# A gated attention unit feeding a feed-forward layer, on one core: doubling the staged z on ScalarE, loading u of two chunks on SyncE's queue, and moving four block sums into the next chunk

## The chip, the cores and the metric

The kernel runs on one core of one Trainium2 chip. The metric is device time in microseconds for one execution. Before the change it took 1172.94 us (median of three runs, 1172.82 to 1172.99). The profiled execution that all rows below come from took 1172.72 us, of which 1170.4 us are the span from the first to the last instruction.

A core has four compute engines that run side by side and meet only at semaphores: TensorE (PE: matmuls, and PEld: its weight loads), VectorE (DVE), ScalarE (ACT) and GpSimd (POOL). SyncE (SP) issues DMA transfers; POOL and ACT can issue them too. Each engine works through its own list of instructions in order, so an instruction that waits holds up all that stand behind it on the same engine.

## The reference

Eight sequences of 3008 tokens go through an attention whose scores are squared after a ReLU, without a softmax; the result is gated by `u` and goes through a feed-forward layer with a sigmoid-approximated GELU:

```python
# u, v: (8, 3008, 256)   z: (8, 3008, 64)   w_in: (256, 2048)   w_out: (2048, 256), all float32
scores = (1.0 / S) * np.matmul(z, z.transpose(0, 2, 1))
attn = np.maximum(scores, 0.0) ** 2
x = u * np.matmul(attn, v)            # (8, 3008, 256), then taken as (24064, 256)
h = x @ w_in
g = h * (1.0 / (1.0 + np.exp(-1.702 * h)))
out = g @ w_out                       # (24064, 256)
```

## The kernel before

**Tiling.** A batch (one of the eight sequences, `b` = 0 to 7) is cut into six chunks of 512 tokens (`NCH` = 6; the last chunk has 448) and into 24 blocks of 128 keys. For each chunk the kernel computes scores z zT (line 247, tile `sc`), applies the ReLU on ACT (line 260, `rl`) and squares on DVE (lines 266 to 297, `a`). Scores are symmetric, so a block that is needed the other way round is turned by a DMA transpose on SP's queue (line 323, `tt`). Then come attn times v (line 651, `o`) and the gate with u (`xt`).

**Three forms of one product.** In the batches 1 to 6 the chunks 3 and 4 use a scheme with seven instead of eight block products (`attend_rows` for chunk 3, `attend_split` for chunk 4). It needs sums and differences of attention blocks (`sa`, lines 418 to 436) and of value blocks (`vt`), all on DVE. Chunk 4 is the place of this change: `split(b, i)` is true for chunk 4 of the batches 1 to 6. It has 42 steps of two 256-column matmuls each (line 483, tile `oz`). Its partial results are copied out of PSUM by ACT (line 495, `ya`) and added up and gated by DVE (lines 497 to 505).

**The feed-forward layer is woven in.** One up-group (`up_group(b, q)`) is four matmuls of x w_in (line 706, tile `hg`, one of two PSUM buffers), the activation on ACT (line 719, `hg` to `gf`, two buffers), and a scaled cast to float16 (`gf` to `gt`), on DVE (line 725) or for chosen `q` on ACT (line 723). Sixteen up-groups (`LAGY` = 16, those of the chunks 0 and 1) run inside chunk 4, one every 2.4 steps; the other up-groups run after chunk 5, between the products with w_out (`pair_product`, line 879, tile `st`). These products use a seven-product scheme too, so the `gt` tiles need block sums on DVE: S1 (line 841), S2 (line 843), S4 (line 845) and S3 (line 836). The sums stand in a list, `SUMS`, in the order S1, S2, S4, S3, and `some_sums(most)` takes one from it, or two when more than `most` wait. Before the change, `up_group` calls it for q from 8 with q % 4 < 2 in chunk 4, which puts three S1 and two S2 on DVE late in chunk 4.

So an up-group is a loop of three engines: PE needs a free `hg`, which ACT frees; ACT needs a free `gf`, which the cast frees; the cast stands in DVE's list among sums, gates and transposes.

**Other work on the queues in chunk 4.** At step 4, POOL first executes a tiny copy, `hold` (line 1120), which waits until the last attention transposes have landed. Then, in this order, POOL issues four transfers of u for chunk 4 (`load_u`, line 207), four of z for the next batch (lines 160 and 163, into two staging tiles `zst`), copies each staging tile once within itself so that z stands there twice (line 174, 128x768 float16), and later issues four transfers of u for chunk 5. The second z tile takes the buffer of an output tile and waits for DVE's transpose `yo` of it (line 981). After each copy on POOL, SP issues a DMA transpose of the staging tile into `ZT` (line 175), and then the stores of `yo` (line 991), four in the odd batches and twelve in the even ones. The tile `ZT` is read by the score matmuls of the next batch, which begin at step 2 of chunk 5; the second half of `ZT` is read from step 41 on. DVE transposes u of chunk 4 (line 214, `ut`) at step 25 and u of chunk 5 at step 8 of chunk 5.

The order on every engine is the order in which the Python code emits the instructions (a manual schedule); there is no planner that moves them. Tables such as `TURNS` and `LOADS` map (chunk, step) to the work that is emitted there.

Of the kernel before, what the change touches and what calls it, by code (L numbers as in the profile page):

```python
# [15 lines left out]
def kernel(  # L16
# [13 lines left out]
    AF = mybir.ActivationFunctionType  # L30
# [6 lines left out]
    NJ = (S + P - 1) // P  # L37
# [3 lines left out]
    NCH = (S + CH - 1) // CH  # L41
    CB = CH // P
    NU = NJ // 2
# [121 lines left out]
    def load_z(b):  # L165
        ZT[b] = pz.tile([P, NJ, P], F16, name="ZT", tag="ZT")
        if b == 1:
            stage_z(b, NU, tag="y")
        if b > 1:
            for n0 in range(0, NJ, NU):  # L170
                stage_z(b, n0, tag="y")
        for n0 in range(0, NJ, NU):
            zst = ZS[n0]
            pool.tensor_copy(zst[:, :, 1, :], zst[:, :, 0, :])
            sp.dma_start_transpose(ZT[b][:, n0:n0 + NU], zst.rearrange("p n c d -> p (n c d)"))

    VB = 4

# [19 lines left out]
        return CH if i < NCH - 1 else LAST  # L198

    def load_u(b, i):  # L200
        eng = pool if b else sp
        n = width(i)
        uq = pu.tile([P, CH // QW, QW, NCC], F32, name="uq", tag="uq")
        src = u[b, i * CH:i * CH + n].rearrange("(q t) c -> t q c", t=QW)
        for k in range(P // QW):
            cs = slice(k * NCC * QW, (k + 1) * NCC * QW)
            eng.dma_start(uq[k * QW:(k + 1) * QW, :n // QW].rearrange("t q c k -> t q (c k)"), src[:, :, cs])  # L207
        UQ[b, i] = uq
# [140 lines left out]
    def split(b, i):  # L349

        return i == NCH - 2 and 0 < b < B - 1
# [339 lines left out]
    def up_group(b, q):  # L691
        s, r = divmod(q, 2 * NFG)
        pair = paired(b, s)
        if pair:
            fg, e = (TILES if q >= 2 * NFG or b else TILES0)[r // 2], r % 2
            if fg >= NFG // 2:
                e = 1 - e
            k = 2 * s + e
        else:
            k, fg = divmod(q, NFG)  # L700
        i, n = blocks(b)[k]
        hg = ps2.tile([P, FFG, CH], F32, name="hg", tag="ps2")
        for e in range(FFG):
            ff = fg * FFG + e
            for c in range(NCC):
                pe.matmul(  # L706
                    hg[:, e, :n], W1[:, c, ff * P:(ff + 1) * P], XT[b, i][:, c, :n],
                    start=(c == 0), stop=(c == NCC - 1),
                )
        if pair:  # L710
            if r % 2 == 0:
                GT[b, s, fg, "pair"] = pa.tile([P, FFG, 2, CH], F16, name="gt", tag="tt", bufs=14)
            g = GT[b, s, fg, "pair"][:, :, k % 2, :n]
        else:
            if fg % 2 == 0:
                GT[b, k, fg // 2] = pa.tile([P, CB, CH], F16, name="gt", tag="tt", bufs=14)
            g = GT[b, k, fg // 2][:, (fg % 2) * FFG:(fg % 2 + 1) * FFG, :n]
        gf = pw.tile([P, FFG, CH], F32, name="gf", tag="gf")
        act.activation(gf[:, :, :n], hg[:, :, :n], AF.Gelu_apprx_sigmoid, scale=1.0 / FSC)  # L719
        if pair and q >= LAGY:  # L720
            some_sums(3 if q % 2 else 8)
        if (q >= LAGY and q % 8 in (1, 3, 5)) or (split(b, NCH - 2) and q in (9, 13)):
            act.activation(g, gf[:, :, :n], AF.Copy, scale=FSC)  # L723
        else:
            dve.tensor_scalar(g, gf[:, :, :n], FSC, None, ALU.mult)  # L725
        if not pair or LAGY > q >= (LAGY // 2 if split(b, NCH - 2) else 0) and q % 4 < (2 if split(b, NCH - 2) else 3):
            some_sums(8)
        if pair:
            some = (("S1", "S2", "S3"), ("S4",))[r % 2] if fg >= NFG // 2 else ()
            SUMS.extend([(s, "S1 S2 S4 S3".index(m), lambda m=m: pair_sum(b, s, fg - NFG // 2, m)) for m in some])  # L730
            SUMS.sort(key=lambda x: x[:2])
            if r == 2 * NFG - 2 and s == NCH // 2 - 1:
                some_sums(8)
        elif fg in (NFG - 3, NFG - 1):
            SUMS.extend([(s, 0, x) for x in left_sums(b, k, fg == NFG - 1)])
# [258 lines left out]
                )  # L994

    LAGY = 2 * NFG
    HEAD = 2

    def pieces(b, i):
# [31 lines left out]
    }  # L1031
    CASTW = {(3, 8): 0, (3, 40): 2, (4, 8): 1, (4, 14): 3}
    LOAD = {(3, NJ + 20): 4, (4, NJ + 5): 5}
    LOADS = {(4, 4): 4, (4, NJ + 5): 5}

    FIRST_ZT, FIRST_CAST = {12: 4, 20: 5}, {5: 4, 13: 5}
    SCHED0 = {
# [45 lines left out]
    for b in range(B):  # L1083
# [7 lines left out]
        for i in range(NCH):  # L1091
# [6 lines left out]
            for n, step in enumerate(  # L1098
                attend_split(b, i) if split(b, i) else attend_rows(b, i) if rowed(b, i)
                else attend(b, i, b == 0 and i == 0)  # L1100
            ):
                if b == 0 and i == 0 and n in (5, 24):
                    load_u(0, n // 24)
                if b == 0 and i == 0 and n == 2:
                    copies = first_zt(3)
                if b == 0 and i == 0 and n == 3:
                    copies()
                if b == 0 and i == 0 and n in FIRST_CAST:
                    first_cast(FIRST_CAST[n], True)
                if b == 0 and i == 0 and n in FIRST_ZT:  # L1110
                    first_zt(FIRST_ZT[n])()
                if (i, n) in turn:
                    turn_u(b, turn[i, n])
                if (i, n) in ((3, 4), (4, 7) if more else (4, 14)) and LAST2:
                    LAST2.pop(0)()
                if (i, n) == (0, 22) and COPY:
                    COPY.pop(0)()
                if split(b, i) and n == 4:
                    hold = pw.tile([P, 2], F16, name="hold", tag="hold")
                    pool.tensor_copy(hold, TT[b, i, NCH - 1][:, ::2, 0, 0])  # L1120
                if (i, n) in load:
                    load_u(b, load[i, n])
                if b == 0 and (i, n) in CASTW:
                    cast_w(CASTW[i, n])
                if b == 0 and (i, n) in LOADW:
                    load_w(LOADW[i, n])
                if b == 0 and (i, n) == (NCH - 2, 6):
                    stage_z(1, 0, tag="yo", bufs=1)
                if more and (i, n) == (NCH - 2, 4 if b else 16):
                    load_z(b + 1)  # L1130
                if b == 0 and i == NCH - 1 and n in (8, 30, 42):
                    wsums.pop(0)()
                take(host, sched[i].get(n, 0))
                if split(b, NCH - 2):
                    for op in extra.get((i, n), ()):
                        op()
                if split(b, i):
                    step()
                if i == full(b) and n >= HEAD and (n - HEAD) * LAGY // (2 * NJ - 10) >= head and head < LAGY:
                    up_group(b, head)  # L1140
                    head += 1
                if not split(b, i):
                    step()
# [64 lines left out]
```

## Time and profile before

| | |
|---|---|
| median of three runs | 1172.94 us |
| profiled execution: time, span | 1172.72 us, 1170.4 us |
| PE busy | 1161.1 us, 99% of the span |
| DVE busy | 983.6 us, 84% |
| ACT busy | 894.9 us, 76% |
| POOL busy | 224.4 us, 19% |
| granted TensorE clock | 1.000 |

The rows of the profile give, for a group of equal instructions, the line, the engine, the operation, output and inputs by tile name, the shapes and the count; after the first bar the busy time in us and the mean of one in ns; after the second bar the idle time of the engine just before them and what ended it. The timeline gives the start and the duration in us, and consecutive equal instructions are merged. Busy PE is not the same as PE at full pace: the ends of matmuls are modelled and overlap the next one (a 512-column matmul is shown with 379 ns, but four of them start within 0.86 us), so a short delay between two matmuls is only seen in the distance of their starts. The view by windows gives for each stretch its length and the busy time of each engine in it.

Chunk 4 of the batches 1 to 6 starts (first matmul of line 483) at 203.8, 348.9, 491.8, 637.0, 780.3 and 925.4 us.

### The profile page before, as it was taken

Reading aid. Unit: us, or ns where it says so; the run is one execution under the profiler, and the core shown is the slowest. Engines: PE = TensorE matmul, PEld = TensorE weight load, DVE = VectorE, ACT = ScalarE, POOL = GpSimd, SP = SyncE. Lnnn points to the kernel's source line nnn. Section 1 sums busy time; section 2 is a strip of 40 time slices with the busy share of each in tenths; the row PEclk is TensorE's granted clock in tenths of the full one; section 3 lists DMA queues with packets and bytes.
Section 4 is the critical chain, followed back from the end, with each engine's and each line's share of the span. In section 5 each row is a group of like instructions: output and inputs, shape, how many; then the busy total and the mean of one; then the engine's idle time right before and its main releaser. Section 6 shows DMA issues by size and latency. Waiting matters only on the chain.

```text
span 1170.4 us, 22657 instructions
## 1 busy us (share of the span) xinstructions
PE 1161.1 (99%) x8656; PEld 611.3 (52%) x8656; DVE 983.6 (84%) x1680; ACT 894.9 (76%) x1043; POOL 224.4 (19%) x307
## 2 busy tenths in 40 slices
PE   9999999999999999999999999999999999999998
PEld 3544456544465445654446545575444654544446
DVE  6779879988799887999879997899978999664776
ACT  7888867788667887688876887768878688672785
POOL 3033200432004320042101431024210251001000
PEclk9999999999999999999999999999999999999999
DMA  9996399754996559976498655987559875698023
GB/s 219 202 161 106 81 174 156 101 91 94 173 151 100 91 108 173 144 111 88 96 166 157 104 87 109 175 140 109 88 106 173 135 118 83 118 171 138 1 37 73
DMA packets 459036, 143.59 MB, mean 123 GB/s; under 512 B 424624, under 2 KB 453040, under 8 KB 458928
## 3 DMA queue, kind: packets, MB, share of 16 engines
q1 hardware_dynamic: 402464, 102.36, 53.4%
q0 software_dynamic: 55104, 38.49, 20.5%
q8 instruction: 67, 1.10, 0.4%
q10 hardware_dynamic: 1360, 1.31, 0.4%
q14 instruction: 41, 0.34, 0.1%
HBM read 60.29 MB, written 24.64 MB: 73 GB/s over the span
## 4 chain that ended last, share of the span: by engine, by line
PE 84%; DVE 11%; ACT 2%; issue 2%; DMA 1%; DVEq 0%; ACTq 0%
PE o L651 29%; PE st L879 23%; PE hg L706 23%; PE sc L247 5%; DVE gt L725 3%; PE oz L483 1%; DVE sa L436 1%; ACT rl L260 1%; PE st L927 1%; DVE sa L430 1%; DMA tt<-a 1%; DVE yo L981 1%; PE yp L853 1%; DVE sa L432 1%; DVE tt L418 1%
## 5 line engine op out<-in xcount | busy, mean ns | idle before, releaser
L719 ACT ACTIVATE gf<-hg 128x1024 f32<-128x1024 f32 (+1 forms) x384 | 380.5, 1001 | 97.2 <-PE hg L706 64.1
L260 ACT ACTIVATE rl<-sc 128x1024 f16<-128x1024 f32 (+1 forms) x344 | 310.8, 941 | 132.1 <-PE sc L247 113.1
L706 PE MATMUL hg<-xt,W 128*128 128x512 f16 (+1 forms) x1408 | 353.4, 374 | 2.1 <-ACT gf L719 1.6
L651 PE MATMUL o<-a,V 64*128 64x512 f16 (+3 forms) x2110 | 271.8, 368 | 0.2 <-DVE a L291 0.2
L651 PEld LDWEIGHTS <-V 64*128 64x128 f16 (+1 forms) x3246 | 174.5, 94 | 174.3 <-issue 5.5
L725 DVE TENSOR_SCALAR gt<-gf 128x1024 f16<-128x1024 f32 (+1 forms) x276 | 193.6, 705 | 59.4 <-ACT gf L719 57.8
L706 PEld LDWEIGHTS <-W 128*128 128x128 f16 x1536 | 149.5, 98 | 160.0 <-issue 6.7
L291 DVE TENSOR_TENSOR a<-rl 128x1024 f16<-128x1024 f16 (+1 forms) x230 | 152.2, 670 | 65.7 <-ACT rl L260 64.6
L207 POOL DMA_DIRECT2D uq<-in_u_dram x168 | 121.0, 730 | 348.1 <-DVE ut L214 157.4
L651 PE MATMUL o<-tt,V 64*128 64x512 f16 (+1 forms) x906 | 119.4, 376 | 0.0
L247 PE MATMUL sc<-ZT 64*128 64x512 f16 (+3 forms) x688 | 117.9, 356 | 0.7 <-ACT ZT L145 0.4
L879 PEld LDWEIGHTS <-WT 128*128 128x128 f16 x736 | 72.0, 98 | 79.6 <-issue 0.6
L723 ACT ACTIVATE gt<-gf 128x1024 f16<-128x1024 f32 (+1 forms) x108 | 110.7, 1025 | 3.6
L879 PE MATMUL st<-gt,W 128*128 128x512 f16 (+1 forms) x368 | 89.9, 370 | 0.0
L879 PE MATMUL st<-s,WT 128*128 128x512 f16 (+1 forms) x368 | 89.1, 370 | 0.0
L879 PE MATMUL st<-gt,WT 128*128 128x512 f16 (+1 forms) x368 | 88.7, 370 | 0.0
L879 PEld LDWEIGHTS <-W 128*128 128x128 f16 x552 | 53.8, 98 | 58.2
L1120 POOL COPY hold<-tt 128x2 f16<-128x2 f16 x6 | 1.6, 265 | 428.2 <-DMA tt<-a 283.3
L896 DVE SCALAR_TENSOR_TENSOR y<-st,y 128x512 f32<-128x512 f32 (+1 forms) x69 | 45.8, 664 | 19.6 <-PE st L879 18.7
L843 DVE TENSOR_TENSOR s<-s,gt 128x1024 f16<-128x1024 f16 (+1 forms) x92 | 60.5, 658 | 0.8
L841 DVE TENSOR_TENSOR s<-gt 128x1024 f16<-128x1024 f16 (+1 forms) x92 | 60.2, 660 | 0.9
L845 DVE TENSOR_TENSOR s<-gt,s 128x1024 f16<-128x1024 f16 (+1 forms) x92 | 59.4, 663 | 1.6 <-DVE s L843 0.5
(128 smaller groups left out, 1278.8 us busy)
## 6 DMA issues: line engine op xcount, KB each, us to landing
out_dram<-yo SPq DMA_DIRECT2D x156, 128.0 KB, 2.8
uq<-in_u_dram POOLq DMA_DIRECT2D x140, 128.0 KB, 3.4
V<-in_v_dram POOLq DMA_DIRECT2D x35, 256.0 KB, 6.0
tt<-a SPq DMA_TRANSPOSE x232, 3.4
uq<-in_u_dram POOLq DMA_DIRECT2D x28, 112.0 KB, 4.9
out_dram<-yo SPq DMA_DIRECT2D x28, 96.0 KB, 4.5
uq<-in_u_dram SPq DMA_DIRECT2D x20, 128.0 KB, 4.3
wst<-in_moe_w_in_dram POOLq DMA_DIRECT2D x4, 512.0 KB, 6.1
```

Source lines behind the costliest of these rows:

```text
L207: eng.dma_start(uq[k * QW:(k + 1) * QW, :n // QW].rearrange("t q c k -> t q (c k)"), src[:, :, cs])
L247: pe.matmul(sc[:, r, :q1 - q0], zt[h, 2 * kp + r, :], zt[h].rearrange("d n p -> d (n p)")[:, q0:q1], start=True, stop=True,)
L260: act.activation(rl[:, :, :n], sc[:, :, :n], AF.Relu, scale=csc)
L291: dve.tensor_tensor(a[:, :, :n], rl[:, :, :n], rl[:, :, :n], ALU.mult)
L651: ins = pe.matmul(acc[c][:, :n], channels(V16[b][h, j], c), weights(b, i, j)[h], start=(k, m) == first[c], stop=(k, m) == final[c],)
L706: pe.matmul(hg[:, e, :n], W1[:, c, ff * P:(ff + 1) * P], XT[b, i][:, c, :n], start=(c == 0), stop=(c == NCC - 1),)
L719: act.activation(gf[:, :, :n], hg[:, :, :n], AF.Gelu_apprx_sigmoid, scale=1.0 / FSC)
L723: act.activation(g, gf[:, :, :n], AF.Copy, scale=FSC)
L725: dve.tensor_scalar(g, gf[:, :, :n], FSC, None, ALU.mult)
L841: dve.tensor_tensor(s_, a21, a22, ALU.add)
L843: dve.tensor_tensor(s_, ST[b, s, "S1", m], a11, ALU.subtract)
L879: pe.matmul(bank, right[:, ff], lhs[:, f], start=new and ff == 0, stop=ff == NFF // 2 - 1, skip_group_check=True,)
```

## The change

It has three parts, all in the batches 1 to 6.

1. The two copies that double the staged z move from POOL to ACT (`twice_z`, emitted at the steps 19 and 28 of chunk 4, each directly followed by its DMA transpose on SP). Batch 0, which stages z for batch 1, keeps the copies on POOL.
2. The eight transfers of u for the chunks 4 and 5 move from POOL's queue to SP's queue. Those of chunk 4 are still emitted at step 4, those of chunk 5 at step 24 instead of 29.
3. No block sum is emitted by `up_group` in chunk 4 any more (`HEADSUMS` is empty). Four S1 sums are emitted in chunk 5, at the steps 18, 22, 26 and 30. The cast of up-group 9 moves from ACT to DVE; that of up-group 13 stays on ACT.

On TensorE the order of all instructions stays what it was. On DVE five sums leave chunk 4 (three S1, two S2), a cast is added there, four S1 are added in chunk 5, and the work after chunk 5 starts with four S2. On SP the order in chunk 4 becomes: u of chunk 4, stores of `yo`, first `ZT` transpose, u of chunk 5, second `ZT` transpose; before it was: first and second `ZT` transpose, stores of `yo`.

```diff
@@ load_z, new function twice_z
         if b > 1:
             for n0 in range(0, NJ, NU):
                 stage_z(b, n0, tag="y")
+            return
         for n0 in range(0, NJ, NU):
-            zst = ZS[n0]
+            twice_z(b, n0)
+
+    def twice_z(b, n0):
+        zst = ZS[n0]
+        if b > 1:
+            act.activation(zst[:, :, 1, :], zst[:, :, 0, :], AF.Copy, scale=1.0)
+        else:
             pool.tensor_copy(zst[:, :, 1, :], zst[:, :, 0, :])
-            sp.dma_start_transpose(ZT[b][:, n0:n0 + NU], zst.rearrange("p n c d -> p (n c d)"))
+        sp.dma_start_transpose(ZT[b][:, n0:n0 + NU], zst.rearrange("p n c d -> p (n c d)"))
@@ load_u
-        eng = pool if b else sp
+        eng = sp if b == 0 or (split(b, NCH - 2) and i >= NCH - 2) else pool
@@ up_group
-        if (q >= LAGY and q % 8 in (1, 3, 5)) or (split(b, NCH - 2) and q in (9, 13)):
+        if (q >= LAGY and q % 8 in (1, 3, 5)) or (split(b, NCH - 2) and q in (13,)):
             act.activation(g, gf[:, :, :n], AF.Copy, scale=FSC)
         else:
             dve.tensor_scalar(g, gf[:, :, :n], FSC, None, ALU.mult)
-        if not pair or LAGY > q >= (LAGY // 2 if split(b, NCH - 2) else 0) and q % 4 < (2 if split(b, NCH - 2) else 3):
+        if not pair or LAGY > q and (q in HEADSUMS if split(b, NCH - 2) else q % 4 < 3):
             some_sums(8)
@@ tables
+    HEADSUMS, LATESUMS = (), (18, 22, 26, 30)
...
-    LOADS = {(4, 4): 4, (4, NJ + 5): 5}
+    LOADS = {(4, 4): 4, (4, 24): 5}
+    TWICE = {19: 0, 28: 1}
@@ the loop over the steps of a chunk
+                if split(b, NCH - 2) and i == NCH - 1 and n in LATESUMS:
+                    some_sums(NCH * NFG)
+                if more and split(b, i) and n in TWICE:
+                    twice_z(b + 1, TWICE[n] * NU)
```

## The prediction

> **What bounds the kernel now.** I read the page first, then the windows of chunk 4, the waits in it, and the timeline of PE, DVE and POOL in batch 2.
>
> ```profile
> span 1170.4 us, 22657 instructions
> PE 1161.1 (99%) x8656; PEld 611.3 (52%) x8656; DVE 983.6 (84%) x1680; ACT 894.9 (76%) x1043; POOL 224.4 (19%) x307
> ```
>
> PE is the bound, and its order does not change. So the change can only move time where PE waits, and I look for those places. The windows run from the first to the last matmul of chunk 4 in the batches 1, 2 and 4:
>
> ```profile
> core 0: us, PE busy (x) PEld busy (x) DVE busy (x) ACT busy (x) POOL busy (x), PEclk, DMA share, GB/s
> 203.80:227.60 23.80, 23.51 (x149) 14.37 (x148) 23.03 (x39) 17.96 (x21) 12.48 (x15) 1.00 0.97 120
> 348.90:373.30 24.40, 23.55 (x151) 14.38 (x148) 23.63 (x40) 17.93 (x21) 11.69 (x15) 1.00 0.83 130
> 637.00:661.80 24.80, 23.78 (x149) 14.29 (x148) 24.03 (x39) 17.93 (x21) 12.21 (x15) 1.00 0.79 122
> ```
>
> The same work takes 23.8, 24.4 and 24.8 us, and DVE is busy for 97% of it (84% over the span). The waits of batch 2 in that window say what follows:
>
> ```profile
> ACT gf L719 <- DVE gt L725: 3.6, 5, 1.0
> PE hg L706 <- ACT gf L719: 0.8, 2, 0.6
> ```
>
> ACT waits for DVE's casts, PE for ACT. PE's loss is larger than these 0.8 us, because modelled ends hide short delays. The starts show it:
>
> ```profile
> 358.06 1.03 PE L706 MATMUL hg<-xt,W 128*128 128x512 f16 x4
> 358.93 0.60 PE L483 MATMUL oz<-sa,vt 128*128 128x256 f16 x4
> 359.70 1.02 PE L706 MATMUL hg<-xt,W 128*128 128x512 f16 x4 [0.17 <-ACT gf L719]
> ...
> 363.60 0.38 PE L483 MATMUL oz<-tt,vt 128*128 128x256 f16 x2
> 364.62 1.02 PE L706 MATMUL hg<-xt,W 128*128 128x512 f16 x4 [0.64 <-ACT gf L719]
> ```
>
> An up-group takes 0.86 us of PE (358.06 to 358.93), a 256-column matmul 0.108 (four between 358.93 and 359.36). So the up-group at 359.70 comes 0.34 us late and that at 364.62 0.81 us late.
>
> Chunk 4 at full pace is 83 x 0.108 + 16 x 0.864 = 22.8 us from its first to its last start. By the starts in the timeline the six batches take 23.77, 24.35, 23.77, 24.84, 23.76 and 24.03 us, 144.5 in all, against 136.7. **The loss that this change can reach is 7.8 us.** It stands in few places: in batch 1 (3 and 5 alike) 0.30 + 0.12 + 0.22 + 0.25, in batch 2 0.34 + 0.81 + 0.13 + 0.20, in batch 4 0.84 early and 1.14 later, in batch 6 0.24 and 0.91. All are ended by DVE, or by ACT behind DVE.
>
> What fills DVE, in batch 2, besides its own sums:
>
> ```profile
> 358.45 0.41 DVE L432 TENSOR_TENSOR sa<-sa,a 128x512 f16<-128x512 f16 x1
> 358.78 0.68 DVE L725 TENSOR_SCALAR gt<-gf 128x1024 f16<-128x1024 f32 x1
> 359.38 1.30 DVE L432 TENSOR_TENSOR sa<-sa,ad 128x512 f16<-128x512 f16 x1
> ```
>
> ```profile
> 359.56 0.83 POOL L174 COPY zst<-zst 128x768 f16<-128x768 f16 x1
> 361.58 1.00 POOL L174 COPY zst<-zst 128x768 f16<-128x768 f16 x1 [1.18 <-DMA zst<-in_z_dram]
> ```
>
> Two equal operations take 0.41 and 1.30 us; the second lies over POOL's copy. Under the second copy a 512-element L436 takes 1.04 us.
>
> **The change, part by part.**
>
> *The z copies leave POOL.* DVE gets back 0.89 + 0.63 us in batch 2, and 2 x 0.63 in batch 1, where two L436 take 1.04 us instead of 0.41. Weighed against the Trainium skill, "SBUF — State Buffer", section "Who interferes with whom": a DVE instruction with two SBUF inputs and a GpSimd instruction that reads SBUF exclude each other for the whole of whichever came first. By that rule the two copies would cost DVE up to their own 0.83 + 1.00 us, 0.3 us more than the rows; the sum would stay, since PE's loss caps it.
>
> *They land on ACT.* The nearest row is a cast of the same width, L723 at 128x768, 843 ns. Two copies are 1.69 us; the cast of up-group 9 (L723, 1.06 us) leaves. ACT goes from 17.9 to 18.6 us of a 22.8 us chunk. The tight place is step 19: between the up-groups 6 and 10 PE needs 5 x 0.86 + 10 x 0.216 = 6.5 us. ACT has five activations (0.91 to 1.02 us apart), two `ya` of 0.38 and the copy of 0.84 there: 6.2 to 6.7 us. Ends: nothing, or the whole 0.84 us per batch. I take 0.15, 0.9 us in six batches, because the two loads are level and ACT's waits for DVE (3.6 us in batch 2) shrink.
>
> The copy adds a wait on ACT: for z to land. Behind it stand the `ya` copy that frees a PSUM bank and all later activations. ACT reaches it about 11.2 us into the chunk. Before, the first z tile landed 10.3 to 11.4 us in (359.23, 214.82, 936.83). But its issue stood behind four u issues of 0.65 us on POOL, which are gone, so 2.6 us earlier. The second copy (step 28, about 16 us in) has z at 12.5 (361.43). Cost: nothing, hidden by those 2 to 3 us.
>
> *u goes to SP.* POOL loses eight issues of about 0.75 us in chunk 4. Casts beside such issues took 0.81 to 0.89 us instead of 0.68, so DVE gains some tenths more; I count none of it. On SP an issue of u takes 0.56 us (its rows of batch 0). SP had nothing to issue between 351.8 and 360.4 in batch 2. Its new order puts four u and up to twelve stores (6.87 us in one stretch of the timeline before) in front of the first `ZT` transpose. In batch 2: `yo` ends 356.33, stores until about 363.3, transpose issued by 364.8 instead of 361.9, landing 3.6 to 8.9 us after issue begins: 367 to 372.3. The first reader is the score matmul at 373.88, some 1.5 us earlier by then, 372.4. So it is hidden, with no margin at the far end. The second half is read only from step 41 on (about 383). u of chunk 5 is issued by 367 and read at 377.27.
>
> *The sums.* Three S1 and one S2 leave DVE in the window, 0.60 us from start to start each, the second S2 at its end; one cast of 0.60 us comes. In front of the last loss (`ya` at 369.90) DVE is ahead by 2 x 0.60 (sums) + 1.52 (copies) - 0.60 (cast) = 2.1 us in batch 2 and by 1.9 in batch 1. The losses behind the first copy are 1.14 and 0.89 us. So they go whole. What is late next is ACT at step 19, above.
>
> *What stays.* 0.34 in batch 2, 0.84 in batch 4 and 0.24 in batch 6 lie before the first copy and before any sum: DVE is behind there by `yo` and by casts of 1.05 and 1.22 us beside POOL's issues. z is still issued on POOL, u is not. Ends: all 1.4 us stay, or none. I take half, 0.7.
>
> *Chunk 5 and after.* Four S1 cost 4 x 0.60 = 2.4 us. In chunk 5 of batch 2 DVE idles 0.73 + 0.23 + 0.39 + 0.18 + 0.32 + 0.33 = 2.2 us behind ACT, and it enters the chunk without the S2 and its lag of about 1 us. So the gates at its end come no later: nothing. After chunk 5 one more sum is left to do than before; an idle gap of 0.85 us at 396.5 takes it. Without that cover it would cost 0.6 us per batch.
>
> Weighed against the move of u, the skill's "DMA: Bandwidth & Descriptors", section "Issuing engines are not separate DMA queues", holds that transfers from any engine end up on the same 16 DMA engines, so that another issuer saves only issue time. The rows: the DMA share in chunk 4 is 0.79 to 0.97 with u on POOL. By the rule the move speeds up no transfer and z would land no earlier than its issue allows; the sum, which counts no faster transfer, is the same.
>
> **Sum.** 7.8 - 0.7 - 0.9 = 6.2 us. The profiled execution took 1172.72 us (span 1170.4), so about 1166.5, with a span of 1164.2. The median of the runs is 0.2 above it: **1166.7 us**.
>
> **The rivals.**
> - *ACT becomes the bound of chunk 4.* For: ACT is level with PE at step 19 and has three `ya` in its list. Against: it idles 5.4 us in batch 2's window, mostly behind DVE. If each first copy costs its whole 0.84 us, 5.0 us come back: 7.8 - 0.7 - 5.0 = 2.1 to, at half that, 4.6 us gained; 1168.3 to 1170.8.
> - *The gain is given back behind chunk 4.* The sums fill DVE in chunk 5, or the first scores wait for `ZT` in the even batches (up to 1.6 us each if the landing takes 8.9 us). For: the margins are 0 to 1 us. Against: S1 is read only by the third product, and the median landing of `ZT` is 5.6 us. Three waits of 1.5 us, or 0.6 us in each of six batches, cost 3.6 to 4.5: 1170.3 to 1171.2.
> - *Slower: ACT stops at the z copy.* One mechanism: z lands late, and ACT, now in order behind it, starves PE of `hg`. The slack is 0.2 us (`ya` ended at 360.86, its bank is written again from 361.86, less the copy's 0.84); each us past it costs nearly 1 us per batch. It decides when z lands 1.7 + 0.2 us after ACT gets there, 13.1 us into the chunk: 10.1 us lost, 7.8 gained, 1175.2 and up. For it: `hold` and `yo` still stand before z. Against: the landings above, 10.3 to 11.4 with a later issue.
> - *It does not do what it says.* DVE's lag comes from its own list and not from what leaves: 0 to 2 us gained, 1171 to 1173. Against: the 0.41 and 1.30 us of two equal rows.
>
> **How the numbers follow.** A difference of 0.2% (2.3 us, faster below 1170.6) is about what a measurement of this kernel can tell from none. Chances: the forecast (1165.1 to 1168.3) 0.68; ACT as the bound 0.14; given back 0.09, two thirds of it still faster; z late 0.04; no effect 0.05. Faster 0.68 + 0.14 + 0.06 = 0.88, same 0.03 + 0.04 = 0.07, slower 0.04 + 0.01 = 0.05. The range: below, the whole 7.8 us and 0.3 for the runs, 1164.8; above, into the ACT case, 1170.0, which leaves out 0.15.
>
> **What would show it.** Right: chunk 4 takes 22.8 to 23.2 us in every batch, DVE about 83% busy in it; no L432 or L436 of 512 elements above 0.5 us; ACT's waits for the cast under 1.5 us; the distance from the last start of chunk 4 to the next batch's chunk 4 unchanged. Wrong: a new idle time of ACT in front of the z copies ended by a DMA; PE waiting for `ya` at step 22; a wait of the first scores for `ZT`; or chunk 5 longer by what chunk 4 lost.

## The result, and the profile after

The changed kernel takes **1166.65 us** (median of 13 runs, 1165.94 to 1171.88); the kernel before took 1173.01 us (median of 13 runs) on the same chip. The medians are 6.4 us apart; the ratio is 0.9952 with a 95% interval of 0.9941 to 0.9963. Ten of the thirteen runs lie between 1165.9 and 1167.1 us and three, of which there is no profile, at 1170.3 to 1171.9; of all executions below one, with u on POOL, took 1344.24 us at a granted clock of 0.85 and is left out. The forecast was 1166.7 us.

The profiled execution took 1165.94 us, its span is 1164.2 us. The first lines of the page, and its chain of work that ended last:

```profile
span 1164.2 us, 22650 instructions
PE 1157.7 (99%) x8656; PEld 611.6 (53%) x8656; DVE 978.5 (84%) x1686; ACT 898.0 (77%) x1049; POOL 178.7 (15%) x247
...
PE 97%; DVE 1%; ACT 1%; issue 0%; SPq 0%; DMA 0%; DVEq 0%; ACTq 0%
```

In the page of before that chain was PE for 84% and DVE for 11%. So nearly nothing that PE waits for is left: DVE's share is gone from the chain although DVE is as busy as before over the span (84%).

Chunk 4 is where the time went. The windows of chunk 4 in the batches 1, 2 and 4, with the columns as before:

```profile
core 0: us, PE busy (x) PEld busy (x) DVE busy (x) ACT busy (x) POOL busy (x), PEclk, DMA share, GB/s
204.00:226.90 22.90, 22.90 (x149) 14.39 (x148) 20.83 (x39) 18.75 (x23) 4.29 (x5) 1.00 0.95 125
348.20:371.20 23.00, 23.00 (x149) 14.40 (x148) 21.05 (x40) 18.65 (x23) 3.82 (x5) 1.00 0.92 130
633.90:657.00 23.10, 23.06 (x148) 14.38 (x148) 21.15 (x40) 18.57 (x23) 4.01 (x5) 1.00 0.94 134
```

From the first to the last start of a split product, the six chunks take 22.88, 22.92, 22.88, 23.11, 22.89 and 23.16 us, 137.8 in all instead of 144.5. That is 6.7 us; the span is 6.2 us shorter (of the other 0.5 us, 0.2 lie ahead of the first chunk 4 and 0.3 behind the last matmul). From the end of one chunk 4 to the start of the next it is 121.35 or 118.53 us, as before to 0.01 us: nothing is given back behind the chunk.

The starts of PE at the place in batch 2 where the up-groups had come 0.34 and 0.81 us late:

```profile
357.36 1.03 PE L713 MATMUL hg<-xt,W 128*128 128x512 f16 x4
358.22 0.60 PE L490 MATMUL oz<-sa,vt 128*128 128x256 f16 x4
358.66 1.02 PE L713 MATMUL hg<-xt,W 128*128 128x512 f16 x4
...
362.59 0.38 PE L490 MATMUL oz<-tt,vt 128*128 128x256 f16 x2
362.81 1.03 PE L713 MATMUL hg<-xt,W 128*128 128x512 f16 x4
```

Every distance is that of full pace: 0.86 for an up-group, 0.44 for four 256-column matmuls, 0.22 for two. DVE and ACT beside it:

```profile
358.34 0.41 DVE L439 TENSOR_TENSOR sa<-sa,ad 128x512 f16<-128x512 f16 x1
358.68 0.68 DVE L732 TENSOR_SCALAR gt<-gf 128x1024 f16<-128x1024 f32 x1
359.28 1.01 DVE L443 TENSOR_TENSOR sa<-tt,sa 128x1024 f16<-128x1024 f16 x2
359.43 0.83 ACT L179 ACTIVATE zst<-zst 128x768 f16<-128x768 f16 x1
360.17 0.38 ACT L502 ACTIVATE ya<-oz 128x256 f32<-128x256 f32 x1
360.43 1.03 ACT L726 ACTIVATE gf<-hg 128x1024 f32<-128x1024 f32 x1
```

L439 (L432 before) with `ad` takes 0.41 us where it took 1.30, and the casts take 0.68. The copy on ACT takes 0.83 us. The `ya` behind it starts at 360.17, 0.05 us after PE has finished its bank: ACT is in time, but only just. In the waits of that window, what ACT loses to DVE's casts:

```profile
ACT gf L726 <- DVE gt L732: 1.2, 2, 0.7
```

It was 3.6 us. What is left of PE's loss are 0.20 us in batch 4 and 0.25 us in batch 6, both 10.6 us into the chunk, behind a cast that lies beside POOL's issue of z (1.01 us in batch 4). A second profile of the same kernel (138.5 us for the six chunks) shows such early losses in the batches 1, 4 and 5 instead, 0.3 to 0.4 us each: where they fall, and how many, differs from one execution to the next.

### The profile page after: what moved, and what is told of

It is laid out like the page before. It is cut to its first block, busy times and chain, and to the rows that moved or that the text cites. A ratio compares the mean times of both kernels' runs of the same rounds, so it can differ in the third digit from the quotient of the medians.

```text
span 1164.2 us, 22650 instructions
## 1 busy us (share of the span) xinstructions
PE 1157.7 (99%) x8656; PEld 611.6 (53%) x8656; DVE 978.5 (84%) x1686; ACT 898.0 (77%) x1049; POOL 178.7 (15%) x247
## 3 DMA queue, kind: packets, MB, share of 16 engines
q10 hardware_dynamic: 1360, 1.31, 0.4%
## 4 chain that ended last, share of the span: by engine, by line
PE 97%; DVE 1%; ACT 1%; issue 0%; SPq 0%; DMA 0%; DVEq 0%; ACTq 0%
PE o L658 30%; PE hg L713 27%; PE st L886 23%; PE sc L254 6%; PE oz L490 4%; PE oz L548 4%; PE st L934 1%; PE yp L860 1%; ACT rl L267 0%; PE w L101 0%; DMA uq<-in_u_dram 0%; SPq L308 0%; DVE gt L732 0%; DVE yo L988 0%; ACT ZT L145 0%
## 5 line engine op out<-in xcount | busy, mean ns | idle before, releaser
L732 DVE TENSOR_SCALAR gt<-gf 128x1024 f16<-128x1024 f32 x282 | 194.8, 691 | 64.8 <-ACT gf L726 62.7
L214 POOL DMA_DIRECT2D uq<-in_u_dram x120 | 84.8, 720 | 382.6 <-DVE ut L221 170.8
L730 ACT ACTIVATE gt<-gf 128x1024 f16<-128x1024 f32 (+1 forms) x102 | 104.4, 1024 | 3.6
```

## The experiments

One number serves for all of them beside the medians: the sum of the six chunks 4 in the profiled execution. It is steadier than a single time, because everything between the chunks takes the same time to 0.01 us in all these profiles, while the stretches ahead of the first and behind the last chunk 4 differ in some, by waits for attention transposes, and a granted clock of 0.50 behind them, that no run here ties to the change (behind the last in the run without the moved sums 5.4 us longer, ahead of the first in the run with u on POOL 9.9 us). It is not exact either: two profiles of the changed kernel give 137.8 and 138.5 us, through their early losses. So a difference of 2 us counts here only where its loss stands at the same place in every batch; the intervals of the ratios of such runs overlap that of the changed kernel (0.9941 to 0.9963). Medians from different groups of runs, as their kernels before show (1173.0 to 1173.6), compare to about 0.6 us.

| kernel | median, us (runs) | before beside it | ratio, 95% interval | six chunks 4, us |
|---|---|---|---|---|
| before | 1173.01 (13) | | | 144.5 |
| z copies alone | 1169.92 (5) | 1173.62 | 0.9963 (0.9949 to 0.9977) | 141.2 |
| sums alone | 1172.03 (10) | 1173.62 | 0.9989 (0.9977 to 1.0001) | 142.3 |
| u alone | 1172.31 (10) | 1173.62 | 0.9989 (0.9980 to 0.9998) | 145.0 |
| the whole change | 1166.53 (4) | 1173.62 | 0.9933 (0.9918 to 0.9948) | 138.5 (137.8 above) |
| whole, z copies on POOL | 1173.33 (10) | 1173.34 | 0.9999 (0.9987 to 1.0011) | 143.4 |
| whole, sums in chunk 4 | 1168.97 (10) | 1173.34 | 0.9968 (0.9954 to 0.9982) | 140.0 |
| whole, u on POOL | 1168.47 (9) | 1173.34 | 0.9964 (0.9938 to 0.9989) | 140.0 |
| before, each POOL copy twice | 1181.44 (4) | 1173.34 | 1.0070 (1.0046 to 1.0093) | 153.2 |
| whole, each ACT copy twice | 1174.98 (10) | 1173.27 | 1.0015 (0.9990 to 1.0040) | 145.7 |
| whole, z issued late | 1191.93 (4) | 1173.27 | 1.0152 (1.0109 to 1.0194) | 163.2 |
| whole, cast 9 on ACT | 1169.86 (10) | 1173.27 | 0.9970 (0.9949 to 0.9991) | 140.1 |
| z copies and cast 9 | 1170.27 (10) | 1173.27 | 0.9969 (0.9951 to 0.9988) | 141.8 |

### The z copies alone

Against the kernel before, the copies move to ACT; u, sums and the cast of up-group 9 stay:

```diff
-            pool.tensor_copy(zst[:, :, 1, :], zst[:, :, 0, :])
+            twice_z(b, n0)
...
+        if b > 1:
+            act.activation(zst[:, :, 1, :], zst[:, :, 0, :], AF.Copy, scale=1.0)
...
+                if more and split(b, i) and n in TWICE:
+                    twice_z(b + 1, TWICE[n] * NU)
```

> The kernel before, with the doubling copies of z on ScalarE as the only part (u stays on POOL, the sums and the casts of the up-groups 9 and 13 stay where they were). Theory (VectorE's lag in chunk 4 costs PE its time, and each part takes some of that lag away): VectorE gets back 1.3 to 1.5 us per batch in front of the last loss, where 0.9 us are lost in the odd batches and 1.1 behind the first copy in the batches 2 and 4. So the losses behind the first copy go (5.9 us), and ScalarE, which keeps the second cast, may take 0.1 to 0.3 us per batch of it: 4.1 to 5.9 us gained, 1167.1 to 1168.9 against 1173.0. Rival (the sums were the load that mattered): 0 to 1.5 us gained. Rival (ScalarE becomes the bound): 0 to 3 us gained, with PE waiting for the copy of the partial result at step 22.

Measured: 3.7 us between the medians, 3.3 us in chunk 4, less than the 4.1 to 5.9 expected. All batches lose 0.35 us some 19 us into the chunk, at the second copy, 2.1 us together; the other 1.8 us are mostly early losses and, in the odd batches, 0.1 to 0.4 us behind the first copy. In the timeline of batch 1:

```profile
220.18 1.06 ACT L730 ACTIVATE gt<-gf 128x1024 f16<-128x1024 f32 x1
221.14 1.00 ACT L726 ACTIVATE gf<-hg 128x1024 f32<-128x1024 f32 x1
222.04 0.83 ACT L179 ACTIVATE zst<-zst 128x768 f16<-128x768 f16 x1
222.78 1.93 ACT L726 ACTIVATE gf<-hg 128x1024 f32<-128x1024 f32 x2
223.84 1.02 PE L713 MATMUL hg<-xt,W 128*128 128x512 f16 x4 [0.18 <-ACT gf L726]
```

ACT works without a gap from the cast of up-group 9 through the copy, and PE waits for it. So the largest part of the change alone does about half of the work, but ACT has no room for copy and cast together.

### The sums alone

Against the kernel before, only the sums move; the cast stays on ACT:

```diff
-        if not pair or LAGY > q >= (LAGY // 2 if split(b, NCH - 2) else 0) and q % 4 < (2 if split(b, NCH - 2) else 3):
+        if not pair or LAGY > q and (q in HEADSUMS if split(b, NCH - 2) else q % 4 < 3):
...
+                if split(b, NCH - 2) and i == NCH - 1 and n in LATESUMS:
+                    some_sums(NCH * NFG)
```

> The kernel before, with the block sums moved from chunk 4 to chunk 5 as the only part (z copies and u stay on POOL, both casts stay on ScalarE). Theory (VectorE's lag): two S1 stand in front of the last loss and one in front of the loss at about 17 us into the chunk, 0.60 us each; so nearly all of the 0.9 us goes in the odd batches and in batch 6, but the 0.81 us loss of the batches 2 and 4 lies before the first sum and stays: 3.5 to 4.3 us gained, 1168.7 to 1169.5. Rival (POOL's copies alone were the cause): 0 to 1 us gained.

Measured: 1.6 us between the medians, with an interval that reaches to no difference; chunk 4 is 2.2 us shorter. The batches 5 and 6 have no loss at all (22.90 us), 1 and 3 lose 0.65 us and 2 and 4 lose as much as before or more (1.8 and 2.0 us), most of it behind the POOL copies. The 3.5 to 4.3 us expected did not come. One thing that differs is where the POOL copies start: 11.3 to 13.7 us into the chunk in 5 and 6, 10.5 to 12.9 in the others. Over every copy one operation of DVE takes 1.04 us or more, in 5 and 6 too.

### u alone

```diff
-        eng = pool if b else sp
+        eng = sp if b == 0 or (split(b, NCH - 2) and i >= NCH - 2) else pool
...
-    LOADS = {(4, 4): 4, (4, NJ + 5): 5}
+    LOADS = {(4, 4): 4, (4, 24): 5}
```

> The kernel before, with u of the chunks 4 and 5 on SyncE's queue as the only part. Theory (VectorE's lag): only the casts beside POOL's issues get shorter, by 0.1 to 0.5 us each; the early losses of the batches 2, 4 and 6 (1.4 us together) shrink and the others stay: 0.3 to 1.5 us gained, 1171.5 to 1172.7. Rival (the order on the queues was what mattered: u and z earlier, the stores before the transposes): 4 us or more gained.

Measured: 1.3 us between the medians (interval 0.2 to 2.3), but chunk 4 of the profiled execution is not shorter (145.0). z lands earlier, so POOL's copies come earlier, and the losses behind them move forward (in the odd batches to 12.3 and 15.4 us into the chunk) instead of going. Where the 1.3 us would lie this profile does not show.

### The whole change beside its parts

The changed kernel again, beside the three on the same chip.

> The changed kernel as it is, for the same chip and the same rounds as its single parts. Every theory expects what it took before: 1166.6, between 1166 and 1167.5. Some of its executions took 1170 to 1172; if that belongs to the chip and not to the execution, all runs here agree among themselves within 0.3%. By the theory of VectorE's lag the parts add up to more than the whole (5 + 4 + 1 against 6.3 us), because each of them is enough for the same losses.

Measured: 7.1 us between the medians. The parts alone make 3.7 + 1.6 + 1.3 = 6.6, so they seem to add up (in chunk 4 less so: 3.3 + 2.2 - 0.5 = 5.0 of 6.0). The next three runs, which take one part away each, show that they don't.

### The whole change with the z copies on POOL

```diff
-        if b > 1:
-            act.activation(zst[:, :, 1, :], zst[:, :, 0, :], AF.Copy, scale=1.0)
-        else:
-            pool.tensor_copy(zst[:, :, 1, :], zst[:, :, 0, :])
+        pool.tensor_copy(zst[:, :, 1, :], zst[:, :, 0, :])
```

with `twice_z` called from `load_z` for all batches, as before the change.

> The whole change without its first part: u on SP and the sums moved as in the changed kernel, but both copies of z on POOL again, directly behind the z transfers. Theory A (the parts add up: alone they brought 3.7, 1.6 and 1.3 us against the runs of the kernel before beside them, 6.6 together, and the whole 7.1): without the copies on ScalarE 3.5 to 4 us are lost, 1169.8 to 1170.6. Chunk 4 then has losses of about 0.6 us per batch, near 1.2 us behind the start of the first copy, behind a VectorE operation that lies over a POOL copy and takes 1.0 us or more instead of 0.41. Theory B (a common lag: VectorE has to be behind by more than a reserve before PE loses anything, and the sums with the u issues free enough reserve): at most 1.5 us lost, 1167 to 1168; the operations over the POOL copies still take 1.0 us or more, but PE's starts show no loss behind them.

Measured: the time of the kernel before (ratio 0.9999). 6.7 us are lost between the medians, more than either theory had; in the profiled execution chunk 4 is 5.6 us longer. In every batch 0.65 to 1.2 us are lost behind the copies. Batch 2, with VectorE's operations over the two copies:

```profile
359.32 1.01 POOL L177 COPY zst<-zst 128x768 f16<-128x768 f16 x1
...
359.57 1.31 DVE L728 TENSOR_SCALAR gt<-gf 128x1024 f16<-128x1024 f32 x1
...
361.74 1.64 DVE L439 TENSOR_TENSOR sa<-tt,sa 128x1024 f16<-128x1024 f16 x2
361.84 1.25 POOL L177 COPY zst<-zst 128x768 f16<-128x768 f16 x1 [1.52 <-DMA zst<-in_z_dram]
361.89 0.38 ACT L498 ACTIVATE ya<-oz 128x256 f32<-128x256 f32 x1
362.05 1.02 PE L709 MATMUL hg<-xt,W 128*128 128x512 f16 x4 [0.40 <-ACT gf L722]
```

The cast takes 1.31 us instead of 0.68, the pair of L439 1.64 instead of 1.01. DVE has five sums less in this chunk and loses all the same. The copies come early here (the first 9.7 to 10.1 us into the chunk, against 10.6 to 11.9 before), and the first sum stood 16.8 us in (batch 2 before). That fits a reserve that stands behind the copies and cannot be spent ahead of time. It also leaves something open: with the sums moved, later copies on POOL cost nothing in two batches (the run with the sums alone), and no run here has the copies on POOL at the steps 19 and 28. So these runs do not part what the other engine brings from what the later place brings.

### The whole change with the sums in chunk 4

```diff
-        if not pair or LAGY > q and (q in HEADSUMS if split(b, NCH - 2) else q % 4 < 3):
+        if not pair or LAGY > q >= (LAGY // 2 if split(b, NCH - 2) else 0) and q % 4 < (2 if split(b, NCH - 2) else 3):
...
-    HEADSUMS, LATESUMS = (), (18, 22, 26, 30)
+    HEADSUMS, LATESUMS = (), ()
```

> The whole change without its third part, except the cast of up-group 9, which stays on VectorE: three S1 and two S2 are in chunk 4 again, none in chunk 5. Theory A (parts add up): 1.2 to 2.0 us lost, 1167.7 to 1168.5, and the loss in chunk 4 stands late, behind up-group 12 (18 us and more into the chunk), where the sums of up-group 8 and on have made VectorE late. Theory B (common reserve, the copies and u free enough of it): 0 to 0.5 us lost, 1166.3 to 1167.

Measured: 2.4 us lost between the medians, 2.2 us in chunk 4. Of these 1.9 us stand at one place, 20.3 to 20.6 us into the chunk, 0.30 to 0.35 us in each of the six batches; neither profile of the changed kernel has them. The waits of PE over the span, and the place in batch 1:

```profile
PE oz L490 <- DVE ya L508: 0.8, 4, 0.2
```

```profile
224.14 0.43 DVE L508 TENSOR_TENSOR ya<-ya,oz 128x256 f32<-128x256 f32 x1
224.21 0.27 PE L490 MATMUL oz<-tt,VZ 128*128 128x256 f16 x1
224.62 0.38 PE L490 MATMUL oz<-tt,vt 128*128 128x256 f16 x2
```

PE needs the bank that the addition of `ya` frees, and DVE comes to it late, after two casts in a row. The matmul starts 0.41 us after the one before it instead of 0.11. Theory A is right in place and, by these 1.9 us, in size (1.2 to 2.0 expected).

### The whole change with u on POOL

```diff
-        eng = sp if b == 0 or (split(b, NCH - 2) and i >= NCH - 2) else pool
+        eng = pool if b else sp
...
-    LOADS = {(4, 4): 4, (4, 24): 5}
+    LOADS = {(4, 4): 4, (4, NJ + 5): 5}
```

> The whole change without its second part: u of the chunks 4 and 5 is issued by POOL again. Theory A: what returns are the early losses that lie before the first copy (0.34 us in batch 2, 0.84 in batch 4, 0.24 in batch 6 before; 0, 0.2 and 0.25 after), 0.8 to 1.4 us: 1167.3 to 1168. In addition z is issued later by four u issues, so ScalarE reaches the first copy before z is there: if that matters, a wait of the first copy for the z transfer shows on ScalarE and each us of it costs up to 1 us in each of six batches, 1169 and up. Theory B (u counts for nothing, as my sum had it): 1166.4 to 1167.

Measured: 1.9 us lost between the medians, 2.2 us in chunk 4; so u seems to count, but this rests on less than the other parts, since the intervals overlap and the early losses vary. In the batches 2, 4 and 6 the early losses are back (0.57, 0.67 and 0.59 us, 1.8 together). In the six profiles here with u on POOL the losses up to 11.1 us into the chunk make 0.9 to 1.8 us, in the eight with u on SP 0 to 1.1 us. Batch 2 of this run shows one, behind a cast beside POOL's issue:

```profile
363.18 1.05 POOL L160 DMA_DIRECT2D zst<-in_z_dram  x1
363.54 1.20 DVE L732 TENSOR_SCALAR gt<-gf 128x1024 f16<-128x1024 f32 x1
...
365.41 0.60 PE L490 MATMUL oz<-sa,vt 128*128 128x256 f16 x4
...
366.19 1.02 PE L713 MATMUL hg<-xt,W 128*128 128x512 f16 x4 [0.18 <-ACT gf L726]
```

In the odd batches 0.1 to 0.4 us are lost some 13 us in. What ACT waited for ahead of its z copies (us in total, times, longest):

```profile
ACT zst L179 <- DMA zst<-in_z_dram: 0.6, 2, 0.4
```

So z issued later by four u issues comes up to 0.4 us too late for ACT in two odd batches. In the changed kernel ACT has no such wait.

### Each copy on POOL twice

```diff
-            pool.tensor_copy(zst[:, :, 1, :], zst[:, :, 0, :])
+            for _ in range(2 if b > 1 else 1):
+                pool.tensor_copy(zst[:, :, 1, :], zst[:, :, 0, :])
```

> The kernel before, with each of the twelve POOL copies of z in the batches 1 to 6 done twice in a row (same result). Theory A (a copy on POOL holds up the VectorE operation with two SBUF inputs that it meets, by 0.63 to 0.89 us, and PE is late by the same, because VectorE has no reserve there): 12 x 0.63 to 12 x 0.89 = 7.6 to 10.7 us more, 1180.5 to 1183.7; less if a copy falls where VectorE works out of PSUM or stands idle, so not under 4 us more. Rival (the operations are long for another reason, the copy only happens to lie beside them): within 1 us of the kernel before, 1172 to 1174.

Measured: 8.1 us more between the medians, 8.7 us more in chunk 4, 0.73 us for each added copy: theory A. In batch 2 (the first line merges four copies, 361.21 to 365.64):

```profile
361.21 4.43 POOL L175 COPY zst<-zst 128x768 f16<-128x768 f16 x4
...
362.69 1.04 DVE L433 TENSOR_TENSOR sa<-sa,ad 128x512 f16<-128x512 f16 x1
363.65 1.31 DVE L726 TENSOR_SCALAR gt<-gf 128x1024 f16<-128x1024 f32 x1
363.78 0.38 PE L484 MATMUL oz<-sa,vt 128*128 128x256 f16 x2 [0.78 <-DVE sa L433]
```

Now PE waits for DVE directly, not only through ACT.

### Each copy on ACT twice

```diff
-            act.activation(zst[:, :, 1, :], zst[:, :, 0, :], AF.Copy, scale=1.0)
+            for _ in range(2):
+                act.activation(zst[:, :, 1, :], zst[:, :, 0, :], AF.Copy, scale=1.0)
```

> The changed kernel with each of the twelve copies of z on ScalarE done twice in a row (same result). Theory A (ScalarE has little room behind the copies: in the changed kernel an activation that follows PE at once leaves about 0.7 us before PE needs its buffer back, up-groups being some 1.3 us apart and hg having two buffers, and the copy already takes 0.3 to 0.4 of it): a second copy of 0.83 us overruns it by 0.1 to 0.5 us, twice in each of six batches, 1.2 to 6 us more than the changed kernel, 1167.7 to 1172.5, with losses of PE behind both copies that end with an activation. Rival (ScalarE idles some 5 us of the chunk and the copies cost PE nothing, once or twice): within 0.5 us of the changed kernel, 1166 to 1167.

Measured: 7.9 us more than the changed kernel in chunk 4, which makes the kernel no faster than before. Theory A holds, but above its range. Batch 1:

```profile
214.74 1.71 ACT L180 ACTIVATE zst<-zst 128x768 f16<-128x768 f16 x2
...
216.36 0.36 ACT L503 ACTIVATE ya<-oz 128x256 f32<-128x256 f32 x1
...
216.78 0.82 PE L491 MATMUL oz<-sa,V 128*128 128x256 f16 x6 [0.39 <-ACT ya L503]
...
220.97 1.71 ACT L180 ACTIVATE zst<-zst 128x768 f16<-128x768 f16 x2
...
223.65 1.02 PE L714 MATMUL hg<-xt,W 128*128 128x512 f16 x4 [0.38 <-ACT gf L727]
```

Two copies take 1.71 us where one takes 0.83, so 0.88 us are added. Behind the first copy PE loses 0.55 us at `ya` and 0.26 us at the next up-group, 0.82 in all (0.91 in the even batches): ACT's reserve there is next to nil. Behind the second it loses 0.54: a reserve of about 0.3 us.

### z issued late

Before the z transfers POOL waits for the `gt` of a later up-group:

```diff
+                if more and split(b, i) and n == 11:
+                    hold2 = pw.tile([P, 2], F16, name="hold2", tag="hold2")
+                    pool.tensor_copy(hold2, GT[b, 0, 4, "pair"][:, 0, 0, :2])
-                if more and (i, n) == (NCH - 2, 4 if b else 16):
+                if more and (i, n) == (NCH - 2, 11 if split(b, i) else 4 if b else 16):
```

> The changed kernel with the issue of z put off: before its z transfers POOL makes a tiny copy that reads a gt tile of a later up-group, so that z lands some 13 us into chunk 4 or later, while ScalarE comes to the first copy 11.2 to 11.7 us in. Theory A (my third rival: ScalarE stands at the copy, with all activations behind it, and PE loses nearly all of what z is late beyond a few tenths): with 1.3 to 1.8 us of waiting in each of six batches, 6 to 10 us more than the changed kernel, 1172.5 to 1176.5, and a wait of ScalarE for the z transfer in the profile. Rival (the wait is absorbed by ScalarE's idle time): under 2 us more, to 1168.5.

Measured: 25.4 us more in chunk 4, 25 us between this median and that of the changed kernel. The mechanism is theory A; z was later than I had aimed for. ACT's wait ahead of its copies, and batch 1:

```profile
ACT zst L179 <- DMA zst<-in_z_dram: 19.0, 6, 3.7
```

```profile
218.00 0.84 ACT L179 ACTIVATE zst<-zst 128x768 f16<-128x768 f16 x1 [2.40 <-DMA zst<-in_z_dram]
218.75 0.37 ACT L502 ACTIVATE ya<-oz 128x256 f32<-128x256 f32 x1
...
219.17 0.82 PE L490 MATMUL oz<-sa,V 128*128 128x256 f16 x6 [2.03 <-ACT ya L502]
```

ACT waited 19.0 us, and PE lost 17.7 us at the `ya` and 6 x 0.26 at the next up-group, 19.3 in all: one us for each us. Some 6.6 us more come from slower matmuls behind the wait in four of the six batches (last section).

### The cast of up-group 9 on ACT

```diff
-        if (q >= LAGY and q % 8 in (1, 3, 5)) or (split(b, NCH - 2) and q in (13,)):
+        if (q >= LAGY and q % 8 in (1, 3, 5)) or (split(b, NCH - 2) and q in (9, 13)):
```

> The changed kernel with only the cast of up-group 9 put back from VectorE to ScalarE. Theory A (ScalarE is what is late next, and the cast had to leave it to make room for the copy): the loss of 0.35 us per batch, some 19 us into the chunk, that the run with the copies alone on ScalarE showed, comes back: 1168.3 to 1169. Rival (that loss came from VectorE's sums, which are gone here, and ScalarE has room for both): within 0.5 us of the changed kernel, 1166 to 1167.

Measured: a loss of 0.35 us in each of the six batches, 19.0 to 19.5 us in, 2.1 us together, that neither profile of the changed kernel has; chunk 4 is 2.2 us longer than in the changed kernel, and the medians are 3.2 us apart. Theory A, at the same place as with the copies alone. In the waits of PE over the span (us in total, times, longest):

```profile
PE hg L713 <- ACT gf L726: 1.1, 6, 0.2
```

### The z copies with the cast, without u and sums

The kernel of the first experiment, and in it

```diff
-        if (q >= LAGY and q % 8 in (1, 3, 5)) or (split(b, NCH - 2) and q in (9, 13)):
+        if (q >= LAGY and q % 8 in (1, 3, 5)) or (split(b, NCH - 2) and q in (13,)):
```

> The kernel before with the copies of z on ScalarE and the cast of up-group 9 on VectorE; u on POOL and the sums as before. Theory A (what the copies alone lacked was room on ScalarE at the second copy): 0.35 us per batch more is gained than by the copies alone (3.7 us), so some 5.5 to 6 us below the kernel before, 1167.3 to 1168 at a kernel before of 1173.3. Theory B (VectorE's own list, with three S1 and two S2 and now one cast more, is then late): 2.5 to 4 us below it, 1169.3 to 1170.8, with the loss some 20 us into the chunk in front of the addition of ya that the run without the moved sums showed (0.30 to 0.35 us per batch).

Measured: 3.0 us below the kernel before between the medians, 2.7 us in chunk 4: theory B. ACT's loss at the second copy is gone, and DVE's at the addition of `ya` has come in its place, 0.35 to 0.45 us in every batch:

```profile
PE oz L490 <- DVE ya L508: 1.3, 6, 0.3
```

**What follows from them together.** Taken away from the whole, the copies cost 5.6 us of chunk 4, the sums 2.2, u 2.2 and the cast 2.2: 12.2 us, where the whole brings 6.7. Against the second profile of the whole it is 4.9 + 1.5 + 1.5 + 1.5 = 9.4 us, where the whole brings 6.0. So the parts need each other. With cast and copy on ACT, ACT is late by 0.35 us; with cast and sums on DVE, DVE is late by as much; only when the sums have left DVE is there room for the cast, and only when the cast has left ACT is there room for the copy. For the first four runs I had expected the opposite, parts of which each alone would cover much of one common lag. That theory fell.

## Why the prediction was right, point by point

**The place and the loss that can be reached.** 7.8 us in the chunks 4, nothing elsewhere. Measured: 6.7 us from chunk 4, nothing between the chunks. My full pace of 22.8 us was a little short: the undisturbed chunks now take 22.88 to 22.92. Against 6 x 22.88 = 137.3 the reachable loss was 7.2 us. The places that I listed one by one add up to 7.3 us, so the 7.8 could have been seen to be too much.

**The copies on POOL.** Confirmed by both signs: a second copy costs 0.73 us each, and with the copies on POOL, directly behind the z transfers, the change brings nothing. The two operations that I showed as 1.30 and 1.04 us take 0.41.

**The losses behind the first copy go whole.** They do. But my working, 2.1 us of lead from sums, copies and cast as one account, is too simple. The runs without one part show separate deadlines: the up-groups behind the copies, and the addition of `ya` 20 us into the chunk. Which share the sums had in the 2.1 us did not matter for the sum.

**ACT at step 19: 0.9 us allowed, nothing lost.** This is the term that was mis-sized. The time that I worked out there, 6.2 to 6.7 us of ACT in 6.5 us of PE, was right as to the room: the doubled copy shows a reserve of next to zero. But a term for "tight" is not a loss; the copy just fits, in every batch. What I had not worked out is step 28, where the cast that leaves ACT decides: 0.35 us per batch.

**What stays: 0.7 us taken of 1.4.** 0.45 us stayed (batches 4 and 6), and the 0.34 us of batch 2 went. In the second profile of the changed kernel 1.1 us stayed, in the batches 1, 4 and 5. The 0.7 lies between the two by choice of the middle, not by working.

**u counted as nothing.** Wrong as an account of its own, as far as one run shows it: with u on POOL chunk 4 takes 1.5 to 2.2 us more, in part by casts of 1.20 us beside POOL's issues (the early losses), in part because z comes late for ACT. The sum held because it took the early losses as half gone without saying by what; the profiles with u on SP have on average less than half of them left.

**z hidden by 2 to 3 us.** It costs nothing, as I said, but the reserve is smaller: in the two profiles of the changed kernel the first z tile lands 1.1 to 2.7 us before ACT comes to its copy. Its issue came some 3 us earlier, about as priced, but it landed only 1.3 to 2.7 us earlier (in the first profile). With z behind the four u issues again, ACT waits up to 0.4 us. Beyond that each us costs one, as the third rival priced it. The rival had the right mechanism and price and did not come about.

**The `ZT` transposes and chunk 5 at nothing.** Right. The first `ZT` transpose of batch 2 landed at 365.9, ahead of my 367 to 372.3, and is read at 371.75. The four S1 left no trace in the distance between the chunks.

**The signs that I named.** No 512-element L439 or L443 above 0.5 us (all 0.41), ACT's wait for the cast 1.2 us, no wait for `ZT`: right. DVE's share of chunk 4 was to be about 83% and is 91% (20.83 of 22.9 us): that figure was wrong, since what leaves is about 2.2 us of 23.0, and the chunk gets shorter too. DVE at 91% without a loss and at 97% with 1 us lost shows how little the share says.

**The sum.** I took 0.6 us too much for what can be reached and kept back 0.9 + 0.25 us too much. Chunk 4 so gave 6.7 us instead of 6.2; the span, with 0.5 us lost outside the chunks, is 6.2 us shorter, as forecast. The place, the mechanism and the size of the loss were worked out; that the number came true to 0.1 us is luck, since three errors of 0.5 us and more cancel in it and two profiles of the same kernel differ by 0.7 us.

## What to carry to other kernels

Before an operation moves from one engine to another, work out the room at its new place from start to start over the few steps around it, not from the share of busy time: here the copy just fitted, and 0.88 us more cost 0.82. And test a change of several parts by taking each part away from the whole as well as by doing it alone; alone they seemed to add up, and only taking them away showed that the sums and the cast had to move for the copies to be worth 5 to 6 us.

## What the runs showed of the hardware

**Casts too are held up by a copy on POOL.** I had put the collision down to operations with two SBUF inputs. In the runs with copies on POOL a cast with one input (128x1024, float32 to float16) took 1.31 us instead of 0.68, as much longer as the additions. The Trainium skill, "SBUF — State Buffer", section "Who interferes with whom", says that a cast or a tensor-scalar operation in a two-port mode takes the shared ports as well; the 1.31 us agree with that. The copies themselves took 0.82 to 1.39 us in the runs that have them on POOL.

**After a wait PE can run at half its clock, and the place of the wait on a fixed grid decides.** In the run with z late the granted clock is 0.50 in four stretches behind the waits, from 220.62, 514.16, 807.71 and 957.90 us on. Each lasts 3.41 us, and they begin 86, 86 and 44 times 3.413 us apart. Windows of that grid at the wait of batch 1 (2.0 us, first two rows) and at that of batch 2 (3.1 us, last three):

```profile
217.20:220.62 3.42, 1.35 (x9) 0.87 (x9) 0.56 (x1) 2.62 (x5) 0.18 (x1) 1.00 1.01 86
220.62:224.03 3.41, 3.41 (x13) 1.48 (x11) 3.41 (x7) 1.62 (x2) 0.00 (x0) 0.50 1.04 184
...
363.98:367.39 3.41, 1.53 (x10) 0.78 (x8) 1.74 (x4) 0.00 (x0) 2.05 (x3) 1.00 1.64 128
367.39:370.81 3.42, 2.10 (x14) 1.35 (x14) 1.30 (x3) 3.36 (x6) 0.00 (x0) 1.00 1.13 143
370.81:374.22 3.41, 3.41 (x23) 2.05 (x22) 3.41 (x6) 3.13 (x4) 0.00 (x0) 1.00 0.87 171
```

In batch 1 PE is idle for 2.1 of the 3.42 us, and 13 matmuls fill the next window where 23 do in batch 2. In batch 2 the longer wait is cut in two by the grid, 1.9 and 1.3 us idle, and the clock stays at 1.00. The other four waits agree: 2.3, 2.6 and 2.1 us idle in one window in the batches 3, 5 and 6, which drop, and 1.6 and 1.4 us in batch 4, which does not. A wait in the run without the moved sums agrees too (2.6 us idle in one window, then 3.41 us at 0.50). So in these runs a window with 2.1 us or more idle is followed by one at half clock, at a cost of about 1.7 us in the chunk, and a window with 1.9 us or less is not. At the losses of 0.1 to 1.1 us that this change removes there was none: the windows of before show a granted clock of 1.00.
